# A sine table transposed by four DMA transposes instead of by TensorE, in an FFT-convolution and token-MLP kernel

## The chip, the cores and the metric

The kernel runs on one core of one Trainium2 chip. The metric is the device time of one execution in microseconds (us), the median of several runs. The core has five engines that run side by side, each in its own program order: TensorE (PE, with its weight loads shown apart as PEld), VectorE (DVE), ScalarE (ACT), GpSimd (POOL) and SyncE (SP). SP, ACT and POOL also issue DMAs; all DMAs share 16 DMA engines.

## The reference, cut to what matters

```python
def _A_ref(q, k, v, shift_k, ssm_k, ssm_D):          # S = 2048, D = 448
    k_shift = sum of 4 shifted copies of k, each scaled by a row of shift_k
    kv = k_shift * v
    kv_f, kf_f = rfft(kv padded to 2S), rfft(ssm_k padded to 2S)
    y = irfft(kv_f * kf_f)[:S] + kv * ssm_D          # a long convolution along the sequence
    return q * y
def _B_ref(x, w1, b1, w2, b2):                       # an MLP over the sequence axis
    u = gelu(einsum("bsd,sf->bdf", layernorm(x), w1) + b1)
    return (einsum("bdf,fs->bds", u, w2) + b2).transpose(0, 2, 1)
x = A_q
h = x + _A_ref(layernorm(x), A_k, A_v, A_shift_k, A_ssm_k, A_ssm_D)
out = h + _B_ref(layernorm(h), B_w1, B_b1, B_w2, B_b2)
```

Inputs and output are bf16.

## The kernel before

The sequence of 2,048 is laid out as 128 partitions by 16 columns (R = 16). Everything in SBUF is one array, `arena`, cut by byte offsets; PSUM is `ps`, eight banks handed out by a pool. The convolution is a Fourier transform in two stages, made of matmuls with sine tables. In order of dependence:

- `tables`: POOL and DVE compute phases, ACT turns them into the sine table `E` (32 blocks of 128 x 128 in fp16, 8 KB per partition), in two halves of 16 blocks (line 820), and smaller tables.
- `loads`: SP issues the loads of ssm_k, k, v and small inputs (lines 860 to 883).
- `kT`, `kv`: PE transposes ssm_k and k, and PE and DVE form the gated kv (DVE line 980).
- `k1`, `u1` (`emit_stage1`): stage one of the two forward transforms, of ssm_k and of kv. Each has four groups i of four steps, `k1.0` to `k1.15`: eight matmuls (L1032), one evacuation by ACT or DVE (L1042; L1040 is the DVE form of group 0 of k), and after every second step three DMAs that shuffle the group's partitions (L1048: two issued by POOL, one by SP). The evacuations write a ring `gring` of four slots; a slot may be written again when the DMAs that read it have landed. The group i = 2 (`k1.8` to `k1.11`) comes first; its slot is next taken by i = 0 (`k1.0` to `k1.3`), whose first evacuation is the DVE operation at L1040. The slot of i = 3 (`k1.12` to `k1.15`) goes to `u1.4`.
- `k2`, `u2` (`emit_stage2`): stage two (L1067), evacuated at L711 to L715.
- `i1` (`emit_products_i1`): the product of the spectra on DVE (L1133), the first inverse stage on PE (L1150), evacuations on ACT (L711), and DMAs that shuffle the result into `TZ` (L1173, issued by POOL and SP; the last step's are L1162).
- `ct0`, `ct` (`emit_ct`): the last inverse stage needs `E` transposed, `ET`. Four times, PE transposes eight blocks into one PSUM bank (L1081) and ACT or DVE copies the bank to `ET`. `ct0.0` is done inside `i1`; `ct.1`, `ct.0`, `ct.2` after it. Four small DMAs (L1100) gather rows of `ET` into `EW`, a table for a correction of the first two columns; two more (L1091) copy zeros.
- `warm`: matmuls whose result is not used (L1183), two of them, between the transposes.
- `i2`: the last inverse stage (L1272, with the correction L1280 for the first two columns), then gating by the layernormed x, the residual and the second layernorm (ACT L1289 and L1327, DVE L1299, L1309, L1358, POOL L1337 to L1351). `xn` (L1242, ACT) prepares the normed x of the first four columns.
- `mlp`: the first matmul (L1405, L1415), GELU on ACT (L1395), the second matmul (L1427), the residual on DVE (L1430) and the stores.

The order of the instructions on every engine is written out by hand in the strings `ORDER["pe"]`, `ORDER["act"]`, `ORDER["dve"]`, `ORDER["pool"]`, `ORDER["sp"]`: a token `ct.1:0-7` is operations 0 to 7 of step `ct.1`. A planner walks these queues with estimated durations; it only decides which PSUM bank or ring slot a step gets, and thereby which earlier readers it must wait for. Each instruction waits by semaphore for what it depends on.

Of the kernel before, what the change touches and what calls it, by code (L numbers as in the profile page):

```python
# [75 lines left out]
    ),  # L76
# [8 lines left out]
    ),  # L85
# [452 lines left out]
def bass_sequential_preLN__ssm_conv_h3__mixer_token_mlp__prompt_kernel(  # L538
    nc,
    A_q,  # L540
    A_k,
    A_v,
    A_shift_k,
    A_ssm_k,
    A_ssm_D,
    B_x,
    B_w1,
    B_b1,
    B_w2,
    B_b2,  # L550
    out,
):
    _build(nc, A_q, A_k, A_v, A_shift_k, A_ssm_k, A_ssm_D, B_w1, B_b1, B_w2, B_b2, out)


def _build(nc, A_q, A_k, A_v, A_shift_k, A_ssm_k, A_ssm_D, B_w1, B_b1, B_w2, B_b2, out):
# [14 lines left out]
    f16 = DT.float16  # L571
# [11 lines left out]
    o_KT = 17024  # L583
    o_W1A = 0
    o_TK = 31360
# [4 lines left out]
    o_E = o_V + 14336  # L590
    o_DG = o_E + 8192
    o_TU = 104064
# [7 lines left out]
    o_ET = 190080  # L600
# [3 lines left out]
    o_IH = o_ID + 256  # L604
# [6 lines left out]
    with ctx:  # L611
        sch = _Sched(nc, ctx, n_dma_sems=112, small_off=SMALL)
        op = sch.op
# [4 lines left out]
        def view(off, shape, dtype=bf16):  # L618
            size = 4 if dtype in (f32, i32) else 2
            n = 1  # L620
            for s_ in shape:
                n *= s_
            ap = AR[:, off // 2: off // 2 + n * size // 2]
            if dtype is not bf16:
                ap = ap.bitcast(dtype)
            if len(shape) == 2:
                ap = ap.rearrange("p (a b) -> p a b", b=shape[1])
            elif len(shape) == 3:
                ap = ap.rearrange("p (a b c) -> p a b c", b=shape[1], c=shape[2])
            return ap  # L630

        KH = view(o_KH, [R, D])
        KT = view(o_KT, [R, D])
# [3 lines left out]
        TK = view(o_TK, [R, 2, D])  # L637
        W1B = view(o_W1B, [R, 896])
        TU = view(o_TU, [R, 2, D])
# [5 lines left out]
        E = view(o_E, [2 * R, 128], f16)  # L645
        ET = view(o_ET, [2 * R, 128], f16)
# [9 lines left out]
        IH = view(o_IH, [128], f16)  # L656
# [24 lines left out]
        psum = _Pool(8, pairs=True)  # L681
# [10 lines left out]
        def Pbf(b, i, dt_=bf16):  # L692
            return PS[:, b.slots[i], :].bitcast(dt_)
# [3 lines left out]
        T_K2, T_U2, T_D2, T_CT, T_BIAS, T_I1, T_DI1 = 45, -11.41, 1.375, 22.37, 56.3, -2.87, 0.974  # L697
# [3 lines left out]
        T_KX = -27.67  # L701
        T_EW = -10.0
        T_CP, T_XL, T_WB = 39.11, -35.53, 156.06
        N_WZ, N_WI, N_W0, N_WK, N_WJ = 2, 0, 9, 3, 0

        def evac(dst, src, w, b, n, scale=None, engs=FX, r=(), est=None):

            def fn(e, W):
                if W == "act":
                    if scale is None:  # L710
                        return e.copy(out=dst(), in_=src())  # L711
                    return e.activation(out=dst(), in_=src(), func=ACT.Copy, scale=scale)
                if scale is None:
                    return e.tensor_copy(out=dst(), in_=src())  # L714
                return e.tensor_scalar(out=dst(), in0=src(), scalar1=scale, scalar2=None, op0=ALU.mult)  # L715
            bs = [b] if b is not None else []
            return op(engs, fn, r=r, w=w, br=bs, n=n, kind="psum", est=est)
# [341 lines left out]
        def emit_stage2(T, o_T, scale):  # L1059
            for jj in range(R // 2):  # L1060
# [10 lines left out]
                for h in range(2):  # L1071
                    i = 2 * jj + h
                    evac(lambda i=i: T[:, i], lambda b=bs[h]: Ppair(b), [(o_T + i * 2 * DB, 2 * DB)], bs[h], 2 * D,
                         scale=scale)

        def emit_ct(late):
            for h in range(1, 4) if late else range(1):
                sch.t0 = T_CT + 0.1 * h
                b = _Buf(psum)
                for i in range(8):  # L1080
                    op("pe", lambda e, W, b=b, h=h, i=i: e.transpose(  # L1081
                        out=Pbf(b, 0, f16)[:, 128 * i:128 * i + 128], in_=E[:, 8 * h + i, :], identity=IH),
                       r=[(o_E + 2048 * h + 256 * i, 256), (o_IH, 256)], bw=[b], kind="tr", safter=i1_last[-1:])
                evac(lambda h=h: ET[:, 8 * h:8 * h + 8, :].rearrange("p a b -> p (a b)"),
                     lambda b=b: Pbf(b, 0, f16), [(o_ET + 2048 * h, 2048)], b, 1024,
                     est={"act": 904.0, "dve": 600.0})
            if not late:
                sch.t0 = T_CT + 1.0
                for jx in range(2):
                    p0 = pz(R // 2 - 1, jx)  # L1090
                    op("sp", lambda e, W, p0=p0: e.dma_start(  # L1091
                        TZ[p0:p0 + 29:4, 0:NZ].rearrange("p r c d -> p (r c d)"),
                        EW[8 * jx:8 * jx + 8].rearrange("p a b -> p (a b)")[:, 0:NZ * D].bitcast(bf16)
                        .unsqueeze(1).broadcast_to([8, 2, NZ * D])),
                       r=[(o_EW, 1024 * NZ)], w=[(o_TZ, NZ * 2 * DB, "zpool")], dmab=8 * NZ * 2 * DB, keng=4, est=660.0)
                for r in range(NZ):
                    for jx in range(2):
                        p0 = pz(R // 2 - 1, jx)
                        q0 = 8 * (R - NZ) + r
                        op("sp", lambda e, W, r=r, jx=jx, p0=p0, q0=q0: e.dma_start(  # L1100
                            EW[q0:q0 + 7 * NZ + 1:NZ, 4 * r + 2 * jx:4 * r + 2 * jx + 2].rearrange("p a b -> p (a b)"),
                            ET[p0:p0 + 29:4, 2 * r:2 * r + 2].rearrange("p a b -> p (a b)")),
                           r=[r_ET(r)], w=[(o_EW + 1024 * r + 512 * jx, 512)], dmab=8 * 512, keng=4, est=660.0)
# [14 lines left out]
        def pz(jj, par):  # L1118
            return 64 * par + 32 * (jj & 1) + (jj >> 1)

        i1_last = []
# [277 lines left out]
        def emit_mlp():  # L1399
# [21 lines left out]
            for r in range(R):  # L1421
# [20 lines left out]
                       r=[(o_X + r * DB, DB)], dmab=128 * DB, rate=400.0)  # L1442

        PLAN = (("dummy", emit_dummy, ()), ("tables", emit_tables, ()), ("loads", emit_loads, ()), ("kv", emit_kv, ()), ("kT", emit_kT, ()),
                ("k1", emit_stage1, (KT, o_KT, TK, o_TK, "k")), ("k2", emit_stage2, (TK, o_TK, 1.0 / 2048.0)),
                ("u1", emit_stage1, (V, o_V, TU, o_TU, "u")),  
                ("xload", emit_xload, ()), ("bias", emit_bias, ()), ("q", emit_q, ()),
                ("u2", emit_stage2, (TU, o_TU, None)), ("ew", emit_ew, ()), ("i1", emit_products_i1, ()), ("ct", emit_ct, (True,)), ("xn", emit_xn, ()), ("w1a", emit_w1_load, (0,)),
                ("warm", emit_warm, (N_WZ, T_I2 - 50.0, lambda: i1_last[-1:])),
                ("i2", emit_i2, ()), ("w1b", emit_w1_load, (1,)), ("w2", emit_w2_load, ()), ("mlp", emit_mlp, ()))  # L1450

# [38 lines left out]
```

## Time and profile before

| | |
|---|---|
| three timed runs, us | 174.57, 174.58, 176.27 |
| median, us | 174.58 |
| span of the profiled execution, first to last instruction, us | 172.8 |
| PE busy | 161.7 us, 94% of the span |
| ACT busy | 89.7 us, 52% |
| DVE busy | 103.2 us, 60% |
| POOL busy | 58.5 us, 34% |
| L1081, the 32 transposes of E on PE | 219 ns each as recorded, pipelined |
| L1048, shuffles issued by SP | 16 of 224 KB, 3.4 us to landing (median) |
| L1173, shuffles issued by POOL | 14 of 196 KB, 4.7 us to landing (median) |

The page gives the profiled execution's time as its span; the median of the runs is 1.8 us longer, which is what lies around the span. The granted TensorE clock is full in all 40 slices of the span. A line of a timeline reads: start in us, length in us, engine, line, operation, output and input shapes, how many, and in brackets how long the engine was idle before and for whom it waited. SPq is the part of SP that issues DMAs.

### The profile page before, as it was taken

What the parts mean: (1) busy time and instruction counts of PE and PEld (TensorE: products, weight loads), DVE (VectorE), ACT (ScalarE), POOL (GpSimd) and SP (SyncE); (2) the same over time, 40 slices, a digit from 0 to 9 for tenths busy, and PEclk for the clock granted to TensorE, in tenths of its full rate; (3) what the DMA queues carried; (4) which work ended last, traced back from release to release, by engine and by line L of the source; (5) the groups of instructions that cost most, each with busy time, mean ns of one, the idle gap of its engine ahead of it and who ended that gap; (6) DMA issues with size and microseconds to landing.
All of it is one profiled execution on the core that took longest, in us unless ns stands there. A gap on an engine that the chain in (4) does not pass through costs nothing.

```text
span 172.8 us, 3570 instructions
## 1 busy us (share of the span) xinstructions
PE 161.7 (94%) x1419; PEld 93.1 (54%) x1419; DVE 103.2 (60%) x191; ACT 89.7 (52%) x129; POOL 58.5 (34%) x152
## 2 busy tenths in 40 slices
PE   6999999989989999848999999999999999999994
PEld 2786755442333233424345555555567777777783
DVE  7998899878989999979897750000003132232231
ACT  3696747898999999979884446321210000000000
POOL 8345727590912524565889630000000000000000
PEclk9999999999999999999999999999999999999999
DMA  5999765783849985456999999930000111101111
GB/s 164 416 314 377 247 202 202 305 332 128 249 108 386 330 266 167 145 168 177 391 396 405 417 423 418 417 156 0 0 0 4 53 53 53 53 0 57 53 53 53
DMA packets 15628, 35.15 MB, mean 203 GB/s; under 512 B 3740, under 2 KB 9740, under 8 KB 15612
## 3 DMA queue, kind: packets, MB, share of 16 engines
q1 hardware_dynamic: 12468, 28.25, 44.9%
q0 software_dynamic: 2880, 6.49, 11.4%
q8 instruction: 11, 0.18, 0.4%
q10 hardware_dynamic: 264, 0.18, 0.3%
q14 instruction: 5, 0.04, 0.1%
HBM read 22.05 MB, written 1.84 MB: 138 GB/s over the span
## 4 chain that ended last, share of the span: by engine, by line
PE 75%; ACT 13%; DVE 5%; DMA 2%; issue 2%; POOL 1%; DVEq 0%
PE ps L1427 24%; PE ps L1415 12%; PE ps L1405 12%; ACT arena L711 9%; PE ps L1032 6%; PE ps L1150 3%; PE ps L1067 3%; PE ps L939 3%; PE ps L998 3%; PE ps L965 3%; PE ps L1011 2%; ACT arena L1042 2%; DMA arena<-arena 2%; DVE arena L980 2%; PE ps L1272 2%
## 5 line engine op out<-in xcount | busy, mean ns | idle before, releaser
L1430 DVE SCALAR_TENSOR_TENSOR arena<-ps,arena 128x448 bf16<-128x448 f32 (+2 forms) x17 | 11.1, 656 | 55.7 <-PE ps L1427 55.7
L1427 PE MATMUL ps<-arena 128*128 128x448 bf16 (+2 forms) x238 | 42.7, 342 | 0.0
L1427 PEld LDWEIGHTS ps<-arena 128*128 128x128 bf16 x238 | 33.3, 145 | 9.5
L711 ACT CAST arena<-ps 128x896 bf16<-128x896 f32 (+1 forms) x31 | 24.9, 945 | 0.7 <-PE ps L908 0.3
L1405 PE MATMUL ps<-arena 128*128 128x448 bf16 x112 | 23.1, 353 | 0.8 <-DVE arena L1347 0.6
L1042 ACT CAST arena<-ps 128x896 bf16<-128x896 f32 x23 | 19.5, 913 | 6.2 <-PE ps L1032 6.1
L1048 POOL DMA_DIRECT2D arena<-arena x32 | 17.5, 553 | 13.4 <-ACT arena L1042 12.9
L1415 PE MATMUL ps<-arena 128*128 128x448 bf16 x112 | 21.7, 352 | 0.0
L1067 PE MATMUL ps<-arena 128*64 128x448 bf16 x128 | 15.9, 360 | 1.5 <-ACT arena L1042 0.4
L1395 ACT ACTIVATE arena<-ps,arena 128x448 bf16<-128x448 f32 x14 | 8.2, 639 | 17.5 <-PE ps L1415 15.1
L1133 DVE TENSOR_TENSOR arena<-arena 128x1792 bf16<-128x1792 bf16 x16 | 16.6, 1085 | 0.9 <-DMA arena<-arena 0.8
L1405 PEld LDWEIGHTS ps<-arena 128*128 128x128 bf16 x112 | 10.6, 98 | 11.8 <-DVE arena L1358 1.6
L1415 PEld LDWEIGHTS ps<-arena 128*128 128x128 bf16 x112 | 11.0, 98 | 10.2
L1150 PE MATMUL ps<-arena 64*128 64x448 bf16 x128 | 14.2, 352 | 1.8 <-ACT arena L711 0.9
L1032 PE MATMUL ps<-arena 128*32 128x448 bf16 x256 | 15.1, 355 | 0.6 <-DVE arena L980 0.3
L1173 POOL DMA_DIRECT2D arena<-arena x14 | 8.2, 589 | 16.4 <-ACT arena L711 16.4
L1327 ACT ACTIVATE arena<-arena 128x448 bf16<-128x448 f32 x14 | 8.1, 575 | 6.8 <-DVE arena L1299 6.6
L1067 PEld LDWEIGHTS ps<-arena 128*64 128x64 f16 x128 | 5.4, 108 | 11.1 <-ACT arena L711 3.8
L1150 PEld LDWEIGHTS ps<-arena 64*128 64x128 f16 x128 | 5.0, 94 | 10.9 <-ACT arena L711 5.3
L1272 PE MATMUL ps<-arena 128*128 128x448 bf16 x32 | 7.7, 353 | 2.3 <-DMA arena<-arena 2.3
L714 DVE COPY arena<-ps 128x1024 bf16<-128x1024 bf16 (+2 forms) x15 | 9.3, 650 | 0.8 <-PE ps L1011 0.7
L1032 PEld LDWEIGHTS ps<-arena 128*32 128x32 f16 x256 | 5.0, 95 | 8.4 <-DVE arena L980 2.6
(96 smaller groups left out, 192.2 us busy)
## 6 DMA issues: line engine op xcount, KB each, us to landing
arena<-in_B_w_dram SPq DMA_DIRECT2D x8, 896.0 KB, 9.8
arena<-in_B_w_dram SPq DMA_DIRECT2D x2, 2048.0 KB, 17.4
arena<-arena SPq DMA_DIRECT2D x16, 224.0 KB, 3.4
arena<-arena POOLq DMA_DIRECT2D x32, 112.0 KB, 3.4
arena<-in_B_w_dram SPq DMA_DIRECT2D x2, 1536.0 KB, 19.1
arena<-arena POOLq DMA_DIRECT2D x14, 196.0 KB, 4.7
arena<-in_A_k_dram SPq DMA_DIRECT2D x4, 448.0 KB, 5.7
arena<-in_A_v_dram SPq DMA_DIRECT2D x4, 448.0 KB, 8.7
```

The source lines that it names most:

```text
L711: return e.copy(out=dst(), in_=src())
L1032: op("pe", lambda e, W, b=b, r=r, q=q, x=x, c0=c0: e.matmul(PS[32 * q:32 * q + 32, b.slots[x], 0:D], E[:, 2 * r + x, c0:c0 + 32], src[:, r ...
L1042: return e.copy(out=dst, in_=Ppair(b)) if W == "act" else e.tensor_copy(out=dst, in_=Ppair(b))
L1048: shuf[tag].append(op(q_, lambda e, W, g=g, i=i, a=a, nu=nu, jh=jh: e.dma_start(T[a + i:a + i + 4 * nu - 3:4].rearrange("p (j k) c d -> p ...
L1067: op("pe", lambda e, W, b=bs[h], h=h, j=j, c=c, par=par: e.matmul(PS[64 * par:64 * par + 64, b.slots[c], 0:D], FW[:, 64 * c:64 * c + 64], ...
L1133: op("dve", lambda e, W, m=m, i=i: e.tensor_tensor(out=MR(m.slots[0]).rearrange("p (x y) d -> p x y d", x=2), in0=TU[:, i].unsqueeze(2).br ...
L1150: k = op("pe", lambda e, W, b=bs[h], m=ms[h], par=par, t=t, tab=tab, xy=xy, P=P: e.matmul(Pb(b, par), tab[P, :], MR(m.slots[0])[P, xy, :], ...
L1272: k = op("pe", lambda e, W, b=b, r=r, h=h: e.matmul(Pb(b), ET[:, 2 * r + h, :], TZ[:, r, h, :], start=(h == 0), stop=(h == 1 and r >= NZ)) ...
L1405: op("pe", lambda e, W, r=r, fc=fc, b=bs[fc]: e.matmul(Pb(b), W1A[:, r, 128 * fc:128 * fc + 128], Q[:, r, :], start=(r == 0), stop=(r == R ...
L1415: op("pe", lambda e, W, r=r, fc=fc, b=b: e.matmul(Pb(b), W1B[:, r, 128 * (fc - n0):128 * (fc - n0) + 128], Q[:, r, :], start=(r == 0), sto ...
L1427: op("pe", lambda e, W, r=r, fc=fc, b=b, d0=d0, d1=d1: e.matmul(Pb(b)[:, d0:d1], W2[fc // 7][:, fc % 7, r:S:R], G[:, fc, d0:d1], start=(fc ...
L1430: op("dve", lambda e, W, r=r, b=b, A=A, d0=d0, d1=d1: e.scalar_tensor_tensor(out=X[:, r, d0:d1], in0=Pb(b)[:, d0:d1], scalar=bm[:, r:r + 1 ...
```

## The change

`ET` is no longer made by PE. A new step `et`, issued by SP directly behind the input loads, transposes `E` into `ET` by four DMA transposes from SBUF to SBUF, each of eight blocks of 128 x 128 fp16 (256 KB). The 32 PE transposes, their four PSUM banks and the four copies (two on DVE, two on ACT) are gone. The unused `warm` matmuls go from two to twelve and stand between the last matmul of `i1` and the first of `i2`. `emit_ct` keeps only the zero copies and the gathers into `EW`; the step that was `ct0.1` is now called `ct0.0`.

```diff
 "pe":
-"... i1.10:10-17 i1.10:1-8 u2.4:0-3 ct0.0:0-7 u2.5:0-3 i1.12:1-8 ..."
-"... i1.16:1-8 i1.16:10-17 ct.1:0-7 warm.0:0 warm.1:0 ct.0:0-7 ct.2:0-7 i2.1:0-1 ..."
+"... i1.10:10-17 i1.10:1-8 u2.4:0-3  u2.5:0-3 i1.12:1-8 ..."
+"... i1.16:1-8 i1.16:10-17 warm.0:0 warm.1:0 ... warm.11:0 i2.1:0-1 ..."
 "act":
-"i1.16:21 ct.0:8 ct.2:8 xn.1:0 xn.2:0 ..."
+"i1.16:21 xn.1:0 xn.2:0 ..."
 "dve":
-"i1.12:0 ct0.0:8 q.3:1 i1.5:0 ... q.4:0 ct.1:8 q.5:2 ..."
+"i1.12:0 q.3:1 i1.5:0 ... q.4:0 q.5:2 ..."
 "sp":
-"... loads.12:0 loads.9:0 loads.7:0 k1.9:11 k1.11:11 k1.13:11 ..."
+"... loads.12:0 loads.9:0 loads.7:0 et.0:0 et.1:0 et.2:0 et.3:0 k1.9:11 k1.11:11 k1.13:11 ..."
...
-        N_WZ, N_WI, N_W0, N_WK, N_WJ = 2, 0, 9, 3, 0
+        N_WZ, N_WI, N_W0, N_WK, N_WJ = 12, 0, 9, 3, 0
...
+        def emit_et():
+            for h in range(4):
+                sch.t0 = -35.0 + 0.1 * h
+                op("sp", lambda e, W, h=h: e.dma_start_transpose(
+                    ET[:, 8 * h:8 * h + 8, :], E[:, 8 * h:8 * h + 8, :].rearrange("p a b -> p (a b)")),
+                   r=[(o_E + 2048 * h, 2048)], w=[(o_ET + 2048 * h, 2048)], dmab=128 * 2048, est=1200.0)
+
         def emit_ct(late):
-            for h in range(1, 4) if late else range(1):
-                sch.t0 = T_CT + 0.1 * h
-                b = _Buf(psum)
-                for i in range(8):
-                    op("pe", lambda e, W, b=b, h=h, i=i: e.transpose(
-                        out=Pbf(b, 0, f16)[:, 128 * i:128 * i + 128], in_=E[:, 8 * h + i, :], identity=IH),
-                       r=[(o_E + 2048 * h + 256 * i, 256), (o_IH, 256)], bw=[b], kind="tr", safter=i1_last[-1:])
-                evac(lambda h=h: ET[:, 8 * h:8 * h + 8, :].rearrange("p a b -> p (a b)"),
-                     lambda b=b: Pbf(b, 0, f16), [(o_ET + 2048 * h, 2048)], b, 1024,
-                     est={"act": 904.0, "dve": 600.0})
             if not late:
...
-                ("kT", emit_kT, ()), ("k1", emit_stage1, ...
+                ("kT", emit_kT, ()), ("et", emit_et, ()), ("k1", emit_stage1, ...
-                ("i1", emit_products_i1, ()), ("ct", emit_ct, (True,)), ("xn", emit_xn, ()), ...
+                ("i1", emit_products_i1, ()), ("xn", emit_xn, ()), ...
```

The planner's walk of the changed queues gives some steps of `u2` and `i1` other PSUM banks: `u2.5` waits for the evacuation `u2.11:5` instead of the later `i1.10:9`, `u2.2` for `u2.5:4`, `i1.12` for `i1.10` instead of `u2.5`. The order of all that remains is the same on every engine.

More of the change, by code (lines that the diff above doesn't have):

```diff
@@ L1444, in _build @@
         PLAN = (("dummy", emit_dummy, ()), ("tables", emit_tables, ()), ("loads", emit_loads, ()), ("kv", emit_kv, ()), ("kT", emit_kT, ()),
-                ("k1", emit_stage1, (KT, o_KT, TK, o_TK, "k")), ("k2", emit_stage2, (TK, o_TK, 1.0 / 2048.0)),
+                ("et", emit_et, ()), ("k1", emit_stage1, (KT, o_KT, TK, o_TK, "k")), ("k2", emit_stage2, (TK, o_TK, 1.0 / 2048.0)),
                 ("u1", emit_stage1, (V, o_V, TU, o_TU, "u")),
                 ("xload", emit_xload, ()), ("bias", emit_bias, ()), ("q", emit_q, ()),
-                ("u2", emit_stage2, (TU, o_TU, None)), ("ew", emit_ew, ()), ("i1", emit_products_i1, ()), ("ct", emit_ct, (True,)), ("xn", emit_xn, ()), ("w1a", emit_w1_load, (0,)),
+                ("u2", emit_stage2, (TU, o_TU, None)), ("ew", emit_ew, ()), ("i1", emit_products_i1, ()), ("xn", emit_xn, ()), ("w1a", emit_w1_load, (0,)),
                 ("warm", emit_warm, (N_WZ, T_I2 - 50.0, lambda: i1_last[-1:])),
```

20 rows, old and new, of the table ORDER are left out of this document.

## The prediction

> **What bounds the kernel now.** I read the chain of waits in order of time first, because the question is whether the removed transposes and copies stand on it. Columns: start, length, what.
>
> ```profile
> 67.10 1.59 ACT arena L711 x2
> 68.69 0.01 issue
> 68.70 2.55 ACT arena L711 x3
> 71.25 0.28 issue
> 71.54 0.58 POOL arena L1173
> 72.12 4.13 DMA arena<-arena
> 76.25 0.05 issue
> 76.30 0.55 PE ps L1272 x2
> ```
>
> The last inverse stage starts at 76.30, released by a shuffle DMA that landed at 76.25; POOL issued that DMA as soon as ACT had evacuated the next-to-last step of the first inverse stage. No L1081 (the PE transposes) is in this chain, nor anywhere else in it. Second, the timeline of the same stretch, to see what lies beside that DMA:
>
> ```profile
> 72.93 1.06 PE L1081 MATMUL ps<-arena 128*128 128x128 f16 x16
> 73.03 0.67 DVE L714 COPY arena<-ps 128x1024 f16<-128x1024 f16 x1
> ...
> 74.47 1.93 ACT L711 COPY arena<-ps 128x1024 f16<-128x1024 f16 x2 [1.34 <-PE ps L1081]
> ...
> 76.28 2.72 ACT L1242 ACTIVATE arena<-arena 128x448 f32<-128x448 bf16 x4
> ...
> 77.65 0.68 DVE L1309 SCALAR_TENSOR_TENSOR arena<-ps,arena 128x448 f32<-128x448 f32 x1 [0.92 <-PE ps L1280]
> ...
> 79.16 1.48 ACT L1289 ACTIVATE arena<-ps,arena 128x448 f32<-128x448 f32 x2 [0.16 <-PE ps L1272]
> ```
>
> Three of the four groups of transposes and three copies lie inside the 4.13 us of the DMA. Behind it DVE and ACT both wait for PE (0.92 and 0.16 us), so the copies do not hold up the next work either. Third, the timelines around the place where SP gets the four new DMAs:
>
> ```profile
> 8.73 3.91 ACT L820 ACTIVATE arena<-arena 128x2048 f16<-128x2048 int32 x2
> ...
> 9.66 0.43 SPq L874 DMA_DIRECT2D arena<-in_A_v_dram  x1
> 16.47 2.53 SPq L1048 DMA_DIRECT2D arena<-arena  x2
> ...
> 25.07 1.08 DVE L1040 TENSOR_TENSOR arena<-ps,arena 128x896 bf16<-128x896 f32 x1
> ```
>
> SP issues its last load at 9.66 and then nothing until 16.47. The second half of E is done at 8.73 + 3.91 = 12.64. L1040 at 25.07 is the first operation that needs SP's shuffles: it writes the ring slot that the first two of them (k1.9, k1.11) read. Fourth, the stretches of 1 us there; the last three columns are granted clock, busy share of the DMA engines, GB/s:
>
> ```profile
> 17.00:18.00 1.00, 1.00 (x28) 0.57 (x24) 1.00 (x3) 0.75 (x2) 1.00 (x2) 1.00 0.51 201
> ...
> 23.00:24.00 1.00, 0.70 (x12) 0.18 (x10) 1.00 (x4) 0.21 (x1) 0.00 (x0) 1.00 0.99 313
> 24.00:25.00 1.00, 0.99 (x22) 0.47 (x22) 1.00 (x2) 0.99 (x2) 0.00 (x0) 1.00 0.41 103
> 25.00:26.00 1.00, 1.00 (x24) 0.24 (x16) 1.00 (x2) 1.00 (x2) 0.00 (x0) 1.00 0.00 0
> ```
>
> The DMA engines are nearly full until 24 us and idle at 25.
>
> **Part by part: what is removed.** The group inside the first inverse stage costs PE 0.62 us at 60.44 and DVE 0.69 us at 62.29. PE waits for ACT on both sides of it (0.36 us before the next step), and ACT runs evacuations without a gap from 60.12 to 66.86, then after 0.24 us of waiting for PE from 67.10 to 73.13. ACT hides it; if everything that PE and DVE gain reached ACT, the gap of 0.24 us would close. That is the whole gain, between 0 and 0.24 us. I take 0: ACT's gap ends with a PE step that itself waited for an ACT evacuation ending at 65.95. The three groups behind the stage cost PE 8 x 3 transposes (72.09 to 73.99), DVE 0.67 and ACT 1.93 us, all covered by the DMA until 76.25. With ACT free at 74.43 the four L1242 can run earlier, but the first consumer, L1309, waits for PE until 77.62, and needs only the first of them, which was done at 76.28 + 0.68 = 76.96: 0.
>
> **The fillers.** Twelve matmuls at the 0.19 us that a 448-column matmul takes back to back here (L1272 pairs in the chain: 0.38), from the end of the last matmul of the stage at 72.16: 72.2 + 2.3, plus some 0.35 us for the last to drain, is 74.8. PE then waits 1.4 us instead of 2.3 for the same DMA: 0. They would cost only if the DMA landed before 74.8.
>
> **The new DMAs: SP's time.** et.0 waits for E until 12.64. Queued behind it on SP are the other three and all 16 shuffles of stage one; POOL's 32 are not behind it. No row shows a DMA transpose. The nearest row is SP's L1048, also SBUF to SBUF, 224 KB: 0.54 us to issue, so four take 2.2 us and SP is free at 14.8, before the 16.47 at which it next has work: 0. From below, the shortest issue on SP is 0.39 us (L871); a gain is excluded, since SP only gets work. From above, SP is held until each transpose has landed: 0.54 + 3.4 us (L1048's landing), 15.8 us in all. What may it take? k1.11's shuffle lands 3.5 us after its issue at that time (2.6 to 4.1), so it must start by 25.07 - 3.5 = 21.57, k1.9's 0.64 us earlier: SP must be free by 20.93, which is 8.3 us after 12.64, 2.1 us for each transpose. Beyond this L1040 is late, and behind it on DVE every evacuation and kv product; DVE is busy for 5.5 of the 6 us from 26 to 32, so most of it passes on. I take 0.54 each, thus 0 for SP's time.
>
> [...]
>
> **The new DMAs: their data.** Four times 256 KB is 1.05 MB. At the 313 GB/s that shuffles reach at a share of 0.99 that is 3.3 us of all engines. Free engine time between 17 and 25 us, summed over these eight stretches as one minus the share (0.51, 0.95, 0.79, 0.92, 0.92, 0.93, 0.99, 0.41): 1.6 us. So 1.7 us of traffic moves past 25. If that is k1.13 and k1.15 (needed by ACT at 28.38) it costs nothing; if the whole 3.3 us lies ahead of k1.11's shuffle (issued at 16.47 + 2.53 - 0.54 = 18.46; plus 3.5 is 22.0, at most 22.6), this lands at 25.3 to 25.9, 0.2 to 0.8 us late. Bounds 0 and 0.8. I take 0.3, because on SP's queue all four transposes do stand ahead of it, and DVE's later gaps (0.20 and 0.55 us) take up a part.
>
> **Sum**: 172.8 + 0 (removed) + 0 (fillers) + 0 (SP) + 0.3 (data) = 173.1 for the span; with the 1.8 us by which the median 174.58 exceeds the span, 174.9.
>
> **The rivals.** First, slower: SP is held by each transpose for longer than the 2.1 us that decide. For it: a transpose cuts its data into many small pieces, and SP's issue in this trace is as long as 0.67 us for the L1173 copies of only 28 KB, so issue time does not go by bytes. Against: nothing on SP shows more than 1 us. At 3.0 us each SP is free at 24.6, 3.7 us late: 178.3; at the bound of 3.94 us it is free at 28.4, 7.5 us late: 182.1.
>
> Second, slower by the data: the transposes move at a third of the shuffles' rate, 10 us of all engines. They start behind the v loads, about 17.5, and k1.11's shuffle lands at about 29, 4 us late: 178.6. For it: the pieces again; against: the shuffles, which also go from partition to partition, run at 313 GB/s, about as fast as the loads (348 to 429 GB/s from 12 to 17 us). [...]
>
> Third, faster: the release at 76.30 was not the DMA but the copies on ACT, which end at 75.4 and 76.4, and with these gone the last inverse stage starts right behind ACT's and POOL's issues at 74.4: up to 1.9 us, 172.7. Against: the landing at 76.25 is measured and is 0.05 us ahead of the matmul, and the only copy that the first matmul needs ended at 75.4.
>
> **How the numbers follow.** Forecast (hidden, or within 0.3 us below and 1.0 above): 62%. SP held 2.1 to 3.0 us each, 175.0 to 178.3: 16%; held longer: 10%. Slow data: 8%. Faster release: 4%. About 1%, 1.75 us, is what a measurement of this kernel can tell from no change: slower than 176.3 are three quarters of the first SP case (from 2.5 us each on), all of the second, and the slow data, 12 + 10 + 8 = 30%; faster than 172.8 the last, 4%; the rest, 66%, is within. The likeliest case's own range is 174.2 to 175.6; the range of 8 in 10 goes from 174.0 to 178.3, leaving out SP's long hold, half of the slow data and the faster release.
>
> **What would show it.** SP's four transposes start at 12.6 and the first L1048 at 16.5: SP's term right; later than 20.9: the first rival. L1040 at 25.1 to 25.9: the data's term; a wait of L1040 or a matmul for a DMA there says how much. DMA share above 0.9 up to 26 or 27. The distance from L1040 to the end (147.7 us) unchanged, the first L1272 still released by the shuffle DMA, 51.2 us after L1040, and PE's clock full. The prediction is wrong if the first inverse stage's ACT chain gets shorter by more than 0.3 us, or if the fillers run past the landing.

## The result and the profile after

| | median | runs | ratio to before, 95% interval |
|---|---|---|---|
| before, on the same chip | 175.14 us (174.57 to 176.27) | 4 | |
| changed kernel | 182.85 us (181.91 to 184.28) | 4 | 1.045 (1.0395 to 1.0504) |

The profiled execution took 182.79 us, 181.0 of it span, against 172.8 before. Here and below medians are over all runs, while ratios leave out runs that were disturbed, so the two need not match exactly.

The page first: granted clock and DMA packets of the changed kernel.

```profile
PEclk9999997599999999997899999999999999999999
DMA packets 19852, 36.20 MB, mean 200 GB/s; under 512 B 7964, under 2 KB 13964, under 8 KB 19836
```

The clock, full in all slices before, drops at two places. The page of before has 15,628 packets and 35.15 MB, 3,740 of the packets under 512 B: the four transposes add 1.05 MB in 4,224 packets, so pieces of some 250 bytes.

The timeline of the changed kernel (start, length, engine, line, operation, and the idle time before with its releaser) at the two places that the prediction watches:

```profile
12.46 11.07 SPq L1079 DMA_TRANSPOSE arena<-arena  x4
23.57 9.52 SPq L1048 DMA_DIRECT2D arena<-arena  x7
29.22 2.09 DVE L1040 TENSOR_TENSOR arena<-ps,arena 128x896 bf16<-128x896 f32 x2 [4.72 <-DMA arena<-arena]
30.36 0.94 PE L1032 MATMUL ps<-arena 128*32 128x448 bf16 x8 [4.79 <-DVE arena L1040]
...
78.44 2.44 PE L1180 MATMUL ps<-arena 128*128 128x448 f16 x12
82.85 0.55 PE L1269 MATMUL ps<-arena 128*128 128x448 bf16 x2 [1.97 <-DMA arena<-arena]
```

SP is in the four transposes until 23.57 and issues its first shuffle there, at 16.47 before. The single holds (the time for which one issue keeps SP) are 1.65, 4.93, 1.36 and 3.00 us. L1040 then waits 4.72 us for a DMA and PE 4.79 us for L1040. Up to that wait this trace runs some 0.6 us ahead of that of before, so L1040 is 4.15 us later than there and not 4.72.

The next two lines are from views of L1048: first SP's first three shuffles in the changed kernel (23.57 to 25.48), then k1.11's shuffle on SP alone in the kernel before, issued at 18.43.

```profile
DMA to landing us min/median/max: 4.7/4.8/4.9
```

```profile
DMA to landing us min/median/max: 2.6/2.6/2.6
```

In the changed kernel k1.11's shuffle is the second, at 24.25. It lands 4.8 us later at 29.05, right ahead of L1040 at 29.22. Before, it landed 2.6 us after its issue, at 21.1, 4.0 us ahead of L1040. The 3.5 us of the prediction is the median of SP's first four shuffles, not this one's time.

The stretches of the changed kernel there (us, busy time of PE, PEld, DVE, ACT, POOL, then granted clock, DMA share, GB/s):

```profile
22.00:24.00 2.00, 1.70 (x38) 0.81 (x32) 2.00 (x5) 0.86 (x1) 0.00 (x0) 1.00 1.38 167
...
26.00:28.00 2.00, 0.00 (x0) 0.00 (x0) 0.00 (x0) 0.57 (x1) 1.08 (x2) 1.00 1.04 392
...
30.00:31.00 1.00, 0.64 (x8) 0.14 (x8) 1.00 (x2) 0.00 (x0) 0.00 (x0) 0.50 0.04 18
```

The share is a mean over the stretch that counts a packet's whole time where the packet starts, so it can pass 1. From 22 to 24 (1.89 and 0.87 in the two single microseconds) the DMA engines are full and yet move only 167 GB/s; shuffles at a share of 0.99 moved 313 in the profile of before. From 26 to 28 PE and DVE do nothing at all. When PE starts again its clock is halved, and it stays so until 36.0, for 6.8 us. The chain of waits of the changed kernel, in order of time, at both places:

```profile
26.05 3.02 DMA arena<-arena
...
29.22 1.10 DVE arena L1040
...
78.42 4.39 DMA arena<-arena
...
82.85 0.55 PE ps L1269 x2
```

The chain puts the wait down to a shuffle of POOL that started at 26.05. The view of that shuffle alone says otherwise:

```profile
DMA to landing us min/median/max: 4.3/4.3/4.3
```

It landed at 30.3, when L1040 had long begun, and POOL's earlier shuffles, the last issued at 21.34, had landed after at most 5.5 us, by 26.9. What L1040 waited for is k1.11's shuffle from SP. In the last inverse stage the shuffle that landed at 82.81 releases the first matmul, as before.

Where the 8.2 us came from, by the starts of the same steps in the two traces:

| | before | after | late by |
|---|---|---|---|
| first L1040 behind SP's shuffles | 25.07 | 29.22 | 4.15 |
| first L1067 | 35.15 | 41.40 | 6.25 |
| first matmul of the last inverse stage | 76.30 | 82.85 | 6.55 |
| the MLP's first group of seven matmuls (L1405, now L1402) | 84.21 | 92.43 | 8.22 |
| end of the span | 172.8 | 181.0 | 8.2 |

Between these steps the stage is as long as before, except in the two stretches where the clock was halved: 2.1 us between the first two rows, 1.7 between the third and the fourth.

### The profile page after: what moved, and what is told of

Same layout as the page of the kernel before. It is cut to its first block, busy times and chain, and to the rows that moved or that the text cites. A ratio compares the mean times of both kernels' runs of the same rounds, so it can differ in the third digit from the quotient of the medians.

```text
span 181.0 us, 3533 instructions
## 1 busy us (share of the span) xinstructions
PE 165.0 (91%) x1397; PEld 93.5 (52%) x1397; DVE 102.3 (57%) x189; ACT 87.5 (48%) x127; POOL 58.6 (32%) x152
## 3 DMA queue, kind: packets, MB, share of 16 engines
q0 software_dynamic: 2880, 6.49, 10.5%
## 4 chain that ended last, share of the span: by engine, by line
PE 69%; ACT 14%; DMA 7%; POOL 3%; DVE 2%; issue 2%; DVEq 0%
PE ps L1424 23%; PE ps L1412 12%; ACT arena L711 11%; PE ps L1402 11%; DMA arena<-arena 7%; PE ps L1032 5%; PE ps L965 4%; PE ps L998 3%; PE ps L1269 3%; PE ps L939 3%; PE ps L1011 2%; POOL arena L1048 2%; ACT arena L1042 2%; PE ps L1067 2%; PE ps L1277 1%
## 5 line engine op out<-in xcount | busy, mean ns | idle before, releaser
L711 ACT CAST arena<-ps 128x896 bf16<-128x896 f32 (+1 forms) x31 | 24.8, 967 | 0.5 <-PE ps L1147 0.2
L1048 POOL DMA_DIRECT2D arena<-arena x32 | 17.6, 555 | 19.8 <-ACT arena L1042 14.7
L1402 PE MATMUL ps<-arena 128*128 128x448 bf16 x112 | 23.1, 353 | 0.8 <-DVE arena L1344 0.6
L1412 PE MATMUL ps<-arena 128*128 128x448 bf16 x112 | 21.7, 352 | 0.0
L1032 PE MATMUL ps<-arena 128*32 128x448 bf16 x256 | 16.2, 376 | 5.3 <-DVE arena L1040 4.8
L1067 PE MATMUL ps<-arena 128*64 128x448 bf16 x128 | 15.4, 360 | 1.7 <-ACT arena L712 0.7
L1402 PEld LDWEIGHTS ps<-arena 128*128 128x128 bf16 x112 | 10.6, 98 | 11.8 <-DVE arena L1355 2.4
L1412 PEld LDWEIGHTS ps<-arena 128*128 128x128 bf16 x112 | 11.0, 98 | 10.2
L1067 PEld LDWEIGHTS ps<-arena 128*64 128x64 f16 x128 | 5.4, 108 | 11.1 <-ACT arena L711 3.6
L980 DVE TENSOR_TENSOR arena<-ps,arena 128x512 bf16<-128x512 f32 (+1 forms) x16 | 9.0, 617 | 3.1 <-PE ps L965 3.1
L1269 PE MATMUL ps<-arena 128*128 128x448 bf16 x32 | 8.5, 383 | 2.0 <-DMA arena<-arena 2.0
## 6 DMA issues: line engine op xcount, KB each, us to landing
arena<-in_B_w_dram SPq DMA_DIRECT2D x8, 896.0 KB, 10.2
```

Source lines behind the costliest of these rows:

```text
L1032: op("pe", lambda e, W, b=b, r=r, q=q, x=x, c0=c0: e.matmul(PS[32 * q:32 * q + 32, b.slots[x], 0:D], E[:, 2 * r + x, c0:c0 + 32], src[:, r ...
L1048: shuf[tag].append(op(q_, lambda e, W, g=g, i=i, a=a, nu=nu, jh=jh: e.dma_start(T[a + i:a + i + 4 * nu - 3:4].rearrange("p (j k) c d -> p ...
L1067: op("pe", lambda e, W, b=bs[h], h=h, j=j, c=c, par=par: e.matmul(PS[64 * par:64 * par + 64, b.slots[c], 0:D], FW[:, 64 * c:64 * c + 64], ...
L1269: k = op("pe", lambda e, W, b=b, r=r, h=h: e.matmul(Pb(b), ET[:, 2 * r + h, :], TZ[:, r, h, :], start=(h == 0), stop=(h == 1 and r >= NZ)) ...
L1402: op("pe", lambda e, W, r=r, fc=fc, b=bs[fc]: e.matmul(Pb(b), W1A[:, r, 128 * fc:128 * fc + 128], Q[:, r, :], start=(r == 0), stop=(r == R ...
L1412: op("pe", lambda e, W, r=r, fc=fc, b=b: e.matmul(Pb(b), W1B[:, r, 128 * (fc - n0):128 * (fc - n0) + 128], Q[:, r, :], start=(r == 0), sto ...
```

## The experiments

Theory A in what follows: each transpose holds SP, so the shuffles behind them are late. Theory B: the transposes' data keeps the DMA engines busy, so the shuffles land late whoever issues them.

**The transposes later in SP's queue.** Two runs move the four steps and nothing else.

```diff
 e1_et_late, "sp":
-"... loads.7:0 et.0:0 et.1:0 et.2:0 et.3:0 k1.9:11 ..."
+"... loads.7:0 k1.9:11 ... u1.15:11 et.0:0 et.1:0 et.2:0 et.3:0 ct0.0:0 xload.2:0 ..."
 e1_et_mid, "sp":
+"... loads.7:0 k1.9:11 k1.11:11 k1.13:11 k1.15:11 et.0:0 et.1:0 et.2:0 et.3:0 u1.1:11 ..."
```

> The four DMA transposes stand on SP behind all shuffles of stage one (behind u1.15), about 45.5 us, instead of ahead of them; nothing else differs from the changed kernel. Theory A (SP's queue is held by the transposes, and the shuffles behind them make L1040 late): L1040 is back at about 25 us, no PE idle of over 1 us before 30 us, clock full there; span about 172.8 to 174, time 174.6 to 176 (the same as before), unless the load of x behind the transposes becomes late (needed at 58 us; then up to 2 us more). Theory B (the 1 MB of the transposes takes the DMA engines wherever it runs, and the traffic after it is late): the loss moves to the load of x and the first inverse stage's shuffles, time still over 178. Theory C (the loss lies in the fillers and the lost TensorE transposes, that is in the clock behind the first inverse stage): time stays above 180.

Measured: 183.09 us (180.19 to 186.27, 4 runs), ratio 1.038 (1.030 to 1.046). L1040 was back at 24.4 and the first L1067 at 34.6, 10.2 us behind it (10.1 in the kernel before, 12.2 in the changed kernel). The loss had moved. Timeline of this run:

```profile
44.72 8.38 SPq L1079 DMA_TRANSPOSE arena<-arena  x4
...
52.18 8.23 DVE L1130 TENSOR_TENSOR arena<-arena 128x1792 bf16<-128x1792 bf16 x8 [3.53 <-DMA arena<-arena]
...
54.44 1.77 SPq L888 DMA_DIRECT2D arena<-in_A_q_dram  x4
...
62.82 1.15 DVE L1206 BATCH_NORM_STATS2 arena<-arena 128x6 f32<-128x448 bf16 x2 [2.41 <-DMA arena<-in_A_q_dram]
```

Here the holds were 2.33, 2.84, 1.77 and 1.31 us. Two waits add up. The x load that stands behind the transposes went out at 54.44, 4.5 us later than the 49.91 of before, and DVE waited 2.41 us for it. Ahead of that, DVE waited 3.53 us (0.82 before) for the last shuffles of stage one. POOL had issued these at 44.90 and 45.43, behind no transpose in its queue; they landed after 5.8 to 6.7 us, where the same two took 4.0 to 4.3 before. The expected guard of up to 2 us covered the x load alone and was too small.

> The four transposes stand on SP behind the first four shuffles (behind k1.15, issued at about 21 us), where the DMA engines run empty from 24 to 26 us. Theory A: k1.9 and k1.11 are on time, L1040 at about 25 us; SP is then held for four transposes without a backlog of loads, 1.4 to 1.7 us each, until about 28 us, so u1.1's shuffle goes out 1 to 2 us late, which has slack until about 33 us: time 174.6 to 176. Theory B: 1 MB has to move between 22 and 28 us in either case, and u1.4 or u1.8 is late by 2 us or more: 177 or more.

Measured: 181.74 us (180.1 to 184.36, 4 runs), ratio 1.038 (1.032 to 1.044). Timeline:

```profile
21.46 7.90 SPq L1079 DMA_TRANSPOSE arena<-arena  x4
...
39.39 1.71 ACT L1042 CAST arena<-ps 128x896 bf16<-128x896 f32 x2 [5.74 <-DMA arena<-arena]
```

Now L1040 is on time (24.8) and what comes next in stage one pays: SP's shuffles go out from 29.40 on, 3 us late, and all those issued from 29.3 to 37 land after 5.3 to 8.1 us (2.2 to 4.7 for those from 26 to 33 before). POOL's, issued from 28.0 to 29.1, took 5.0 to 7.3 us, against 3.0 to 4.7 for the same ones before. So both runs show A and B at once: what stood behind the transposes on SP went out late (4.5 and 3 us), and what was in flight beside them landed late, POOL's too (5.0 to 7.3 us instead of 3.0 to 4.7 in the second).

**The shuffles off SP.** The four shuffles that were late are issued by POOL, the transposes stay early.

```diff
 "pool":
-"... k1.9:9-10 k1.11:9-10 k1.13:9-10 k1.15:9-10 ..."
+"... k1.9:9-11 k1.11:9-11 k1.13:9-11 k1.15:9-11 ..."
```

> The four transposes stay where the change has them, at 12.5 us, but the four shuffles k1.9, k1.11, k1.13, k1.15 that SP issues right behind them are issued by POOL instead. Theory A (the held queue of SP): L1040 back at 25 to 26 us, PE idle there under 1 us, clock full, time 175 to 177. Theory B (the data: the engines are full of transposes until about 26 us, whoever issues the shuffles): L1040 still at 28 us or later, time 180 or more.

Measured: 180.06 us (178.97 to 182.55, 4 runs), ratio 1.0295 (1.0233 to 1.0356). Timeline:

```profile
12.21 12.53 SPq L1079 DMA_TRANSPOSE arena<-arena  x4
...
29.64 2.09 DVE L1040 TENSOR_TENSOR arena<-ps,arena 128x896 bf16<-128x896 f32 x2 [5.03 <-DMA arena<-arena]
```

With k1.9 and k1.11 no longer behind a transpose on SP, L1040 is still at 29.64. The shuffles on POOL between 18.6 and 25.9 landed after 5.6 to 13.2 us (median 10.5). POOL waited seven times, 8.1 us in all, for earlier DMAs to land before it could issue, but only after it had issued k1.11's: the first such wait ends at 22.03. The last part of k1.11's shuffle went out at 20.17, within the 21.57 of the prediction, and the view of it alone reads:

```profile
DMA to landing us min/median/max: 9.4/9.4/9.4
```

It landed at 29.6, and L1040 waited for it. So here B alone is enough: issued in time, the shuffle landed too late. Why POOL's take so much longer than the 4.8 us of SP's in the changed kernel stays open. (The trace is that of the slowest of the four runs, 182.55 us.)

**The price of one transpose by itself.** The kernel of before, with four more transposes of the same 256 KB and then four plain copies of the same bytes, all issued by SP behind the last GELU, where the DMA engines have nothing else to do. Nothing reads what they write.

> The kernel before, unchanged in its work, with four extra DMA transposes of the same size issued by SP behind the last GELU (about 128 us), where the trace of before shows the DMA engines idle, and then four plain DMA copies of the same 256 KB from the same bytes to the same place; nothing reads either. It measures the disputed cost by itself. Theory A (the transposes are ordinary DMAs that only met a full queue at 12.5 us): with the engines idle each transpose lands within 3 to 3.5 us of its issue like a plain copy, SP issues the four within 2.5 us. Theory B (the transpose itself is slow: it moves 256-byte pieces, and the engines do little else meanwhile): SP is still held 1.3 us or more for each, the four take 6 us or more from first issue to last landing, at 170 GB/s or less, against about 4 us for the copies.

Measured once, 177.18 us. The views of the two lines (L1083 the transposes, L1085 the copies; issue time in ns, shortest, median, longest):

```profile
L1083 SPq DMA_TRANSPOSE arena<-arena x4: 1304/1330/1641, 131.1 to 135.2; - x4
...
L1085 SPq DMA_DIRECT2D arena<-arena x4: 497/575/607, 138.6 to 142.1; - x4
```

The stretches of the same run, the first under the transposes, the other two around the first copy:

```profile
132.00:138.00 6.00, 6.00 (x34) 4.60 (x33) 1.37 (x2) 0.00 (x0) 0.00 (x0) 1.00 0.99 177
139.00:140.00 1.00, 1.00 (x7) 0.77 (x6) 0.05 (x1) 0.00 (x0) 0.00 (x0) 1.00 0.23 90
140.00:141.00 1.00, 1.00 (x7) 0.75 (x6) 0.00 (x0) 0.00 (x0) 0.00 (x0) 1.00 0.45 172
```

A transpose holds SP for 1.33 us where a copy of the same bytes holds it for 0.58. The engines are full (share 0.99) at 177 GB/s, so the four keep them busy for 1.05 MB / 177 GB/s = 5.9 us. The first copy, 262 KB, fits into 0.23 + 0.45 = 0.68 us of engine time, 385 GB/s. With idle engines SP is never held for more than 1.64 us, so the 4.93 and 3.00 us of the changed kernel go with what else stood in the queue and on the engines there. Holds of this length are not peculiar to transposes. The kernel before has them where weight loads follow on each other (view of L1382, 896 KB each DMA, issue time in ns as above; four loads of the same size at L1378 from 51.7 to 79.3 us held SP for 0.38 to 0.54 us):

```profile
L1382 SPq DMA_DIRECT2D arena<-in_B_w_dram x4: 769/1706/2292, 79.8 to 84.6; - x4
```

**Plain copies in place of the transposes.** The changed kernel with four plain copies at the same place of SP's queue; the transposition of `E` is left out.

```diff
-op("sp", lambda e, W, h=h: e.dma_start_transpose(
-    ET[:, 8 * h:8 * h + 8, :], ...
+op("sp", lambda e, W, h=h: e.dma_start(
+    ET[:, 8 * h:8 * h + 8, :].rearrange("p a b -> p (a b)"), ...
```

> The changed kernel with four plain DMA copies of the same 256 KB from E to ET at the same early place on SP, instead of the four DMA transposes: the transposition of the table is left out, so the last inverse stage works with an untransposed table. Theory A (it is how a transpose holds SP and works the DMA engines, not its place and bytes): each copy holds SP 0.5 to 0.6 us as in the measurement with idle engines, SP is free at about 15, k1.9 goes out at 16.5, L1040 at 25 to 25.9, time 174.5 to 176.5. Rival (any 1 MB put there does it): SP held until the loads have drained, L1040 at 28 or later, clock halved behind it, time 180 or more.

Measured: 175.0 us (174.01 to 176.41, 10 runs), ratio 0.998 (0.994 to 1.0015). Timeline:

```profile
12.55 2.46 SPq L1079 DMA_DIRECT2D arena<-arena  x4
...
24.62 1.09 DVE L1040 TENSOR_TENSOR arena<-ps,arena 128x896 bf16<-128x896 f32 x1
```

The same bytes at the same place of the queue cost nothing as copies: SP is free by 15.01, and L1040 has no wait. So what the changed kernel loses it loses to the form of the DMA. The megabyte is not free by itself, though. The view of k1.11's shuffle on SP, issued at 17.86, reads:

```profile
DMA to landing us min/median/max: 6.3/6.3/6.3
```

It took longer than in the changed kernel (4.8) and still landed 4.9 us earlier than there, at 24.2, because it went out 6.4 us earlier. Its part on POOL landed last, at 24.5, hardly 0.1 us ahead of L1040. The copies differ from the transposes in two ways: they stay within their partitions, and they add 576 packets, of some 1.8 KB each, instead of 4,224. Which of the two makes the hold was not tested.

**How many early transposes are free.** One, two or three groups by DMA in SP's early place, the rest on PE as before, with the two fillers of before.

> The kernel before, with only the first of the four groups (the one that PE transposed inside the first inverse stage) made by a DMA transpose at the early place; the other three stay on PE, the fillers are two as before. Theory A: SP is held 1.65 us as in the changed kernel's trace, free at 14.1, before its first shuffle at 16.5: time of before within 0.5 us. Theory B: the 256 KB come out of the DMA engines between 14 and 19 us, where they are full with the loads of v; shuffles land up to 1 us later than 22.6, still before the 25.07 at which they are needed: the same.

> As the one with one early group, but two groups by DMA transpose at the early place and two on PE. Theory A: SP is free at 19.1 (1.65 and 4.93 us as in the changed kernel's trace), k1.11's shuffle starts at 19.8 instead of 18.5 and lands at 23.3 to 24.6, before 25.07: time of before within 0.5 us, and the cost of the change sits in the third and fourth transpose. Theory B: half of the 1 MB costs half of the changed kernel's stall of 4.7 us at L1040: 1.5 to 2.5 us, and the clock may fall: 176 to 178.

> The kernel before with three of the four groups by DMA transpose at the early place, and the last on PE. Theory A, a threshold: one and two early transposes left L1040 at 25.0 and 25.1; with three SP is free at about 20.5 (the third starts at 19.1 and holds it 1.4), 0.4 us before the limit of 20.9, but landing takes longer than before beside the transposes (4.8 us instead of 3.5): L1040 at 25.5 to 26.5, time 0.5 to 2 us above before. A smooth cost by bytes instead would have shown in the one and two already, and gives three quarters of the changed kernel's 7.7 us here: 180.

| early | SP free | L1040 | median, runs | ratio, 95% |
|---|---|---|---|---|
| 1 | 14.01 | 24.97 | 176.02 us, 10 | 1.0049 (1.0002 to 1.0096) |
| 2 | 19.13 | 25.13 | 176.74 us, 10 | 1.0028 (0.9977 to 1.008) |
| 3 | 20.52 | 26.96 | 179.86 us, 4 | 1.0253 (1.0175 to 1.033) |
| 4 (the change) | 23.53 | 29.22 | 182.85 us, 4 | 1.045 (1.0395 to 1.0504) |

Timeline of the run with three:

```profile
12.28 8.24 SPq L1079 DMA_TRANSPOSE arena<-arena  x3
...
26.96 2.09 DVE L1040 TENSOR_TENSOR arena<-ps,arena 128x896 bf16<-128x896 f32 x2 [2.54 <-DMA arena<-arena]
```

L1040 is late from three on, so the edge lies between two and three, as expected. The times agree with that, though the interval of one early transpose just leaves out 1, at 0.5%. Three cost 4.6 us by the medians (175.26 before in that set) and not the expected 0.5 to 2. That is the number of the smooth cost by bytes, 180, which the runs with one and two rule out; 1.9 us of it is L1040's, and the clock was halved in two stretches (granted 0.82 in the mean from 30 to 36 us, 0.83 from 76 to 82).

The row with three parts A from B. Its SP was free at 20.52, inside the 20.93 that the prediction allowed, and k1.11's shuffle went out at 21.39, inside 21.57. With the prediction's 3.5 us it would have landed at 24.9, ahead of the 25.07 of before. It took 5.4 us, and L1040 was 1.9 us late.

Both count, then. In the kernel before, k1.11's shuffle landed 4.0 us ahead of L1040. With four transposes it went out at 24.25 instead of 18.43, 5.8 us later, and took 4.8 instead of 2.6 us, 2.2 more. 5.8 + 2.2 - 4.0 = 4.0 of the 4.15 us. By this sum the slower landing alone would have been hidden, and the held queue alone would have cost some 1.8 us.

**More fillers.** Ten more in the changed kernel, to cover PE up to the landing.

```diff
-N_WZ, N_WI, N_W0, N_WK, N_WJ = 12, 0, 9, 3, 0
+N_WZ, N_WI, N_W0, N_WK, N_WJ = 22, 0, 9, 3, 0
```

> The changed kernel with 22 fillers instead of 12, so that they run from 78.4 us until about 82.6, just before the DMA lands for which the last inverse stage waits. If the second stretch of halved clock (83.9 to 87.1 us) comes from the 2 us in which PE is idle behind the fillers, it is gone in the profile and the span is 1.0 to 1.7 us shorter than the changed kernel's 181.0; the first stretch (29.6 to 36) stays. If it is something else, the clock falls there all the same and the time is the changed kernel's.

Measured: 181.68 us (181.28 to 184.61, 4 runs), ratio 1.041 (1.036 to 1.0457); profiled span 179.5. The clock of the page, then the timeline:

```profile
PEclk9999997599999999999999999999999999999999
```

```profile
78.69 4.34 PE L1180 MATMUL ps<-arena 128*128 128x448 f16 x22
83.00 0.55 PE L1269 MATMUL ps<-arena 128*128 128x448 bf16 x2
```

In the profile the second drop is gone (granted clock 1.00 from 82 to 87 us), the first stays (0.50 from 30 to 36), and the MLP's first matmul (ahead of the table's group of seven) starts at 88.68 instead of 90.21: 1.5 us. The medians differ by 1.2 us and their intervals overlap, so the trace shows this gain and the times don't confirm it.

**Taking the holds apart.** Each transpose alone at a place that was thought to have slack on SP, first spread over four places, then in two forms that keep two early and hide the rest.

```diff
 e5_spread, "sp":
+"... k1.15:11 et.0:0 u1.1:11 ... u1.15:11 et.1:0 ct0.0:0 ... i1.8:22 et.2:0 i1.10:20 ... ct0.0:5 et.3:0 i1.6:20 ..."
 e7_hidden3, "sp":
+"... loads.7:0 et.0:0 et.1:0 k1.9:11 ... k1.15:11 et.2:0 u1.1:11 ... i1.16:22 et.3:0 w1a.1:0 ..."
 e7_hidden2, "sp":
+"... loads.7:0 et.0:0 et.1:0 k1.9:11 ... i1.16:22 et.2:0 et.3:0 w1a.1:0 ..."
```

> The changed kernel with the four transposes one at a time: behind k1.15 (21 us), behind u1.15 (45 us), behind i1.8 and behind i1.12 (about 60 and 66 us). Theory A (it is the time for which SP is held in one piece): each hold is 1.3 to 2.3 us, within the slack that every place has; time 174.5 to 176. Theory B (the DMA engines): each transpose delays the shuffles in flight beside it by about its own time of 2 to 3 us, and the places behind u1.15 and in the first inverse stage have little slack: 176 to 179.

Measured: 179.8 us (179.53 to 181.97, 4 runs), ratio 1.027 (1.018 to 1.036). The first, behind k1.15, held SP for 2.04 us and did no harm (L1040 at 25.8). The second stood ahead of the x load again, which went out at 54.15 instead of 49.91. But SP was free of it at 48.57 (46.28 + 2.29). The waits of this run (engine and line, releaser, us in total, times, longest):

```profile
DVE arena L1130 <- DMA arena<-arena: 3.9, 1, 3.9
```

DVE waits for a shuffle to land, and so does SP ahead of the x load (1.9 us in the view of its queue). POOL's last two of stage one, issued at 46.45 and 46.99 beside the transpose and behind none, landed after (view of L1048, POOL):

```profile
DMA to landing us min/median/max: 5.7/6.4/7.1
```

In the kernel before the same two took 4.0 to 4.3 us, and the x load waited for them there too, but only until 49.9. So this is theory B as it was expected at this place, and not the hold: this transpose held SP for no longer than the slack there and still delayed what was in flight beside it.

> All four groups by DMA transpose, put where the traces so far show slack: two at the early place (no cost there), one behind k1.15 at 21 us (landed without harm when it stood there alone), one behind the last shuffle of the first inverse stage at 75 us, where SP waits for landings until 78.3 (it is needed at about 88 us). With theory A (each place has its own slack, and what is within it is free) the time is that of before within 1 us, or up to 0.3 us below. If transposes cost wherever they are (about 2 us each): 178 or more.

> As the one before, but two at the early place and two behind the last shuffle of the first inverse stage, at 75 us. If the shuffle DMAs from POOL, for which the last inverse stage waits until 76.25, are slowed by the transposes in flight from 75 us, the start of that stage moves by up to 2 us: 175 to 177; if not, 174.5 to 175.

Measured: 175.16 us (174.51 to 177.22, 12 runs), ratio 0.9998 (0.9959 to 1.0037), and 175.06 us (174.66 to 175.71, 12 runs), ratio 1.0008 (0.9977 to 1.004). The chain of waits of the second, in order of time:

```profile
72.13 4.21 DMA arena<-arena
...
76.39 0.55 PE ps L1269 x2
```

All four transposes are by DMA here, PE's 32 are gone, and no transpose is in the chain: the last inverse stage starts at 76.39 (76.30 before), released by the same shuffle. So what the change takes away is worth nothing that these times can tell (0.4% is 0.7 us), and no version found beats the kernel before.

## Why the prediction was wrong

It gave 174.9 us (174.0 to 178.3); the time is 182.85. Its likeliest case was "hidden". What came is its first rival, in the part to which it gave 16%: holds of 2.1 to 3.0 us each, with a measured mean of 2.77. It priced that at 175.0 to 178.3; the time came out some 4.5 us above the upper end.

**SP's time: this step failed.** "I take 0.54 each", from a shuffle's issue. That is right for a copy (0.58 us alone, 2.46 for four in the early place, and a time unchanged) and wrong for a transpose: 1.33 us with idle engines, a mean of 2.77 in the loaded queue. The row chosen was the nearest in bytes and in path, and not in the kind of work: the bytes are those of a copy, but they move across partitions in pieces of 250 bytes.

The trace of before could have warned. "Nothing on SP shows more than 1 us" is misread: one issue of L1100 took 1.87 us, and the weight loads at L1382 and L1389 up to 2.29 and 4.01 us, with other DMAs under way. (Nor is 0.39 us the shortest issue; L888 has 0.35. It enters no sum.)

**Its deadline held for SP, but not by itself.** SP free by 20.93, 2.1 us each, puts the edge between two and three early transposes, and there it is. It took 3.5 us for k1.11's shuffle to land, a median of four; k1.11's own 2.6 would have put the deadline 0.9 us later. With three transposes ahead it took 5.4, so SP met the deadline and L1040 was late all the same. The prediction did let the data delay this shuffle, but only for an SP that is free on time.

**The data: the rate was wrong.** "313 GB/s", so 3.3 us of engines, was taken from shuffles. Alone the transposes run at 177 GB/s, 5.9 us. The first rival's 178.3 for a hold of 3.0 us each leaves out that shuffles behind such data land later (4.8 us after issue, not the 3.5 of the sum), and that behind both stalls the clock was at 0.50, for 6.8 and 3.4 us. The second rival supposed a third of the rate; it was 0.57 of it.

**"PE's clock full" was wrong.** The two stalls were followed by 6.8 and 3.4 us at half the clock, 2.1 + 1.7 us by the table of starts. No run took the first drop away and left the stall, so the 2.1 is a difference of the traces and not an isolated price. For the second, the profiled execution of the kernel with two early transposes gives a comparison: its L1067 was on time (35.19) and its last inverse stage started at 76.52, but the clock was halved until 82.2 (0.50 from 76 to 82; by the 0.981 that is its mean over the span, for some 6.7 us) and the span was 175.8, so a drop at that place cost about 2.8 us. It was twice as long as the changed kernel's second one, for which that makes 1.4 us, an estimate.

**What was right.** The removed transposes and copies: 0, shown by the two kernels that hide all four. The fillers don't delay the stage: they ended at 80.88 and the landing was at 82.81. They don't hold the clock in this trace either (0.50 from 84 to 87); PE waited 1.97 us behind them, not 1.4. L1272, now L1269, is still released by the shuffle DMA. The distance from L1040 to the end was to stay at 147.7 us; it became 151.8, the two stretches at half the clock and 0.3 us more. The third rival, a faster release, is out.

## What to carry to other kernels

Price a DMA by its own kind, not by a transfer of the same bytes: with idle engines the transposes held the queue for 2.3 times as long as copies of the same bytes (1.33 and 0.58 us) and moved at 0.46 of their rate (177 and 385 GB/s). A cost that no row shows is best bounded by a look at one such DMA in an idle stretch, and then at its place, where it was twice as long again (2.77 us in the mean). Here the work moved from PE to SP's queue was paid for twice: by what stood behind it there (k1.11's shuffle went out 5.8 us later), so list the issues behind it with their last useful start, and by what was in flight beside it (that shuffle took 4.8 us to land instead of 2.6; beside a single transpose POOL's last two of stage one took 5.7 to 7.1 instead of 4.0 to 4.3), so let the landing times grow as well. Check first that the removed work is on the path at all; here it was not, and the best version only broke even.

## What the runs showed of the hardware

A DMA transpose from SBUF to SBUF (256 KB, 16-bit) holds SP for 1.33 us and lands after 3.1 us with idle engines, at 177 GB/s over all engines, against 0.58 us, 2.4 us and 385 GB/s for a plain copy. Behind loads it held SP for up to 5.2 us (the second of three early ones), and its landing took up to 14.8 us (in the run with shuffles on POOL). For this shape the transpose's rate is less than half of the copy's.

Shuffles in flight beside transposes landed later in stage one, on both queues: POOL's last two after 5.7 to 7.1 us with one transpose beside them and 4.0 to 4.3 us with none, SP's k1.11 after 4.8 us behind four of them and 2.6 with none. Behind four plain copies the latter took 6.3 us. At the end of the first inverse stage it was not so: with two transposes issued by SP from 74.96 on, the shuffle that POOL had issued at 72.13 took 4.21 us, the last 1.4 of them beside these, against 4.13 before.

In the changed kernel 1.97 us of PE's waiting ahead of the last inverse stage were followed by half the clock (0.50) from 83.8 to 87.2; with the ten more fillers over that wait it stayed at 1.00. With plain copies it was halved at this place too (0.72 in the mean from 76 to 82 us). It was not behind 1.9 us with the transposes behind all of stage one (no matmul of L1269 above 363 ns, 581 in the changed kernel), nor behind 2.31 us in the kernel before (1.00), nor with one early transpose (mean of the run 1.00), where the waits of PE and of its weight loads for that DMA add up to 5.4 us, against 4.4 in the changed kernel. So the length of the wait alone doesn't decide. The halved stretch at this place was 3.4 us long in the changed kernel and some 6.7 with two early transposes. No run moved the gap by itself, so the cause stays open.
